# A chunked delta rule ahead of a two-layer projection on one core: merge pieces of two blocks joined, masks moved to GpSimd, a 48-row state update

## The chip, the cores and the metric

The kernel runs on one core of a Trainium2 chip. The metric is device microseconds (us) of one execution; the figure to forecast is that of the changed kernel. Engines are named as in the profile: PE (TensorE, with PEld for its weight loads), DVE (VectorE), ACT (ScalarE), POOL (GpSimd) and SP (SyncE, which issues most transfers).

## The reference

4 batches of 8 heads, 768 steps, head size 48. Per head a 48x48 state is read by the query and then corrected by the key (delta rule). The result, 3072 tokens of 384 numbers, goes through two matrix products with a clipped square between them.

```python
k_n = k / (norm(k) + 1e-06)
for t in range(S):
    y[:, :, t] = einsum('bhd,bhde->bhe', q[:, :, t], state)
    v_old = einsum('bhde,bhd->bhe', state, k_n[:, :, t])
    state = state + beta[t] * einsum('bhd,bhe->bhde', k_n[:, :, t], v[:, :, t] - v_old)
x = y.transpose(0, 2, 1, 3).reshape(B * S, H * D)
h = x @ w_in
g = where(h >= 1, h, where(h <= -1, 0, (h + 1) ** 2 / 4))
out = g @ w_out
```

## The kernel before, in words

The 768 steps are cut into 12 blocks of 64, and blocks go in 6 pairs, G = 0 to 5. Within a block all 32 heads are worked at once (16 units side by side on two halves of the 128 partitions). Per block the kernel makes the Gram matrix of the keys (`gram_k`), inverts the triangular 64x64 system that the Gram matrix and beta define, makes the query Gram matrix and masks it (`gram_q`), and then runs the chain through the state: `chain_r` (the old state's part taken off the values), `chain_u` (the inverse applied), `chain_y` (the output y), `chain_d` (the state's update).

The inverse is made in two steps. DVE solves 32x32 systems of both blocks of a pair together (`solve_whole`, 30 steps of two operations, lines 358 and 360), scales and transposes the result into `XT` and `GG` (`unlanes_whole`, lines 366, 368, 371). PE then joins the 32x32 parts into 64x64 with two products per block (`merge32`): y1 = GG·XT, whose negative ACT writes to `GG`, and x2 = GG·GG, which ACT writes to `XT`.

The other work is the projection, in 102 items. Pair 0 has 22 items, every later pair 16. An item is `up` (9 matmuls of 512 columns into a PSUM buffer h, of which there are two), then ACT's Relu (line 826) and Square (838), DVE's min/max that reads h a last time (840), ACT's cast to ghi (805), DVE's rest glo (806), and `down` (12 matmuls of 384 columns), which runs two items later. So `up` of an item may begin only when line 840 of the item two before has read its h. In this document "the min/max" means line 840.

While the items of pair G run, the inverse and the chain of pair G+1 are woven in. The order is written by hand: `plan(G)` puts pieces for PE into the table `pe` and steps for the other engines into the table `fill`, at times counted in items; each item has two half-steps. In this document "half-step n" counts within the 32 half-steps of one pair's 16 items. A PE piece of an even half-step stands between `up` and `down` of its item, one of an odd half-step behind `down`. Every engine works its list in that order. A piece's PSUM comes from a ring of two banks named `ch`; a piece that needs both waits until the pieces before it have been read out.

In pairs worked by `plan(1)` to `plan(4)` (blocks 4 to 11) the pieces are: `chain_r` of the first block at half-step 5, `gram_q` at 9 and 12, three merge pieces at 17, 18 and 22, `gram_k` of the next pair at 19 and 24, and `chain_u`, `chain_y`, `chain_d`, `chain_r`, `chain_u`, `chain_y`, `chain_d` at 20, 21, 23, 25, 27, 28, 30. The solve begins three half-steps before the pair's own first item.

Of the kernel before, what the change touches and what calls it, by code (L numbers as in the profile page):

```python
# [7 lines left out]
F32 = mybir.dt.float32  # L8
# [5 lines left out]
C = 64  # L14
NP = 4
D = 48
# [24 lines left out]
def delta_rule_moe(ctx: ExitStack, tc: tile.TileContext, kqa, kqb, kv, beta, w, out):  # L41
# [202 lines left out]
    def gram_q(g):  # L244

        x, b_ = Q[g], banks(C)
        for j in range(H):
            for e, f in quarters():
                r, o = slice(f * C, f * C + D), other(e, f) * C
                nc.tensor.matmul(b_[e][o:o + C, j], K[g][r, e * H + j, :], x[r, (1 - f, 1)[e], e * H + j, :], start=True, stop=True)  # L250

        def moved():
            for o in range(2):
                yield x[o * C:o * C + C, o, 0:H], b_[0][o * C:o * C + C], slice(o * C, o * C + C)
            yield x[:, 0, H:NU], b_[1], slice(0, P)

        def evict():
            def raw():
                for a, b, r in moved():
                    nc.scalar.copy(out=a, in_=b)  # L260

            def masks(copied=False):
                for a, b, r in moved():
                    nc.vector.tensor_tensor(out=a, in0=a if copied else b, in1=mask[r, None, :].broadcast_to([r.stop - r.start, H, C]), op=ALU.mult)  # L264
                    yield
            return (raw, masks(True)) if g < 2 else lambda: run(masks())
        return evict

    def norms(n, out):
# [93 lines left out]
    def unlanes_whole():  # L363

        A, gm = S["A"], S["gm"]
        nc.vector.tensor_tensor(out=A, in0=A, in1=gm[:, None, :].broadcast_to([P, 32, 32]), op=ALU.mult)
        yield
        nc.vector.transpose(out=XT[:, :, :, 32:64].rearrange("p g u t -> p t (g u)"), in_=A.rearrange("l c t -> l t c"))
        yield
        for g in range(2):  # L370
            nc.vector.transpose(out=GG[:, g, :, 32:64], in_=XT[:, g, :, 32:64])
            yield
# [44 lines left out]
    def merge32(ga, gb, first=False):  # L417
# [10 lines left out]
        def evict():  # L428
# [3 lines left out]
            if ga is not None:  # L432
# [7 lines left out]
                for r in (0, C):  # L440
                    (nc.vector.tensor_copy if first else nc.scalar.copy)(out=XT[r:r + 32, ga, :, 0:32], in_=XT[r:r + 32, ga, :, 32:64])
        return evict

    def chain_r(g):
        b_ = banks(D)
# [111 lines left out]
    def chain_d(g):  # L557
        b_ = banks(D)
        keys = KV[g].rearrange("p h u d -> p (h u d)")
        for j in range(H):  # L560
            for e, x in quarters():
                r, o, k = slice(x * C, x * C + C), other(e, x) * C, e * H + j
                n = C if e else D
                nc.tensor.matmul(b_[e][o:o + n, j], keys[r, k * D:k * D + n], SU[r, (x, 0)[e], k, :], start=True, stop=True)  # L564

        def moved():
            for f in range(2):
                yield SU[f * C:f * C + D, 1 - f, 0:H], b_[0][f * C:f * C + D]
            yield SU[:, 1, H:NU], b_[1]

        def evict():
            if g == 0:
# [22 lines left out]
    def run(gen, n=99):  # L595
        for _ in range(n):
            if next(gen, 0) == 0:
                break
# [130 lines left out]
    def at(where, G, t, *x):  # L729
        where.setdefault(2 * first[G] + int(round(2 * t)), []).extend(x)  # L730
# [10 lines left out]
    def plan(G):  # L741
# [11 lines left out]
        else:  # L753
# [8 lines left out]
            t, n = (MERGE / 2 + 7 - FT - HALF, 31 + 2 * HALF - MERGE) if G == 1 else (-1.5, 17)  # L762
# [12 lines left out]
        chain(G, M + 1.5, a)  # L775
        if G < NS - 2:
            if G:
# [119 lines left out]
```

## Time and profile before

| | before |
|---|---|
| three runs | 593.45, 595.01, 601.75 us |
| median of them | 595.01 us |
| the profiled execution | 594.22 us |
| its span, first to last instruction | 592.5 us |
| mean granted clock of TensorE | 0.991 |
| PE, DVE, ACT, POOL busy | 574.1, 393.6, 327.3, 32.9 us |

The span is what the rows below are measured in, counted from its start; 1.7 us lie around it. A busy PE is not PE at its peak, since matmuls are pipelined: what a stretch of PE costs is read here from one start to the next start. In the timeline neighbouring rows of one line and form are merged, and the mean granted clock close to 1 means that nearly all of the span ran at 2.4 GHz.

### The profile page before, as it was taken

What the parts mean: (1) busy time and instruction counts of PE and PEld (TensorE: products, weight loads), DVE (VectorE), ACT (ScalarE), POOL (GpSimd) and SP (SyncE); (2) the same over time, 40 slices, a digit from 0 to 9 for tenths busy, and PEclk for the clock granted to TensorE, in tenths of its full rate; (3) what the DMA queues carried; (4) which work ended last, traced back from release to release, by engine and by line L of the source; (5) the groups of instructions that cost most, each with busy time, mean ns of one, the idle gap of its engine ahead of it and who ended that gap; (6) DMA issues with size and microseconds to landing.
All of it is one profiled execution on the core that took longest, in us unless ns stands there. A gap on an engine that the chain in (4) does not pass through costs nothing.

```text
span 592.5 us, 21657 instructions
## 1 busy us (share of the span) xinstructions
PE 574.1 (97%) x9585; PEld 498.0 (84%) x9585; DVE 393.6 (66%) x827; ACT 327.3 (55%) x587; POOL 32.9 (6%) x67
## 2 busy tenths in 40 slices
PE   8898899999999999999999999999999999999996
PEld 6677788789978888888888898888888888899986
DVE  5977999854689934699924699924699924323332
ACT  4648876467544385534385544385544374454443
POOL 6200010000020000010000010000010000000000
PEclk9988999999999999999999999999999999999999
DMA  5674766100343011144011144001143000020001
GB/s 146 195 254 147 202 225 198 56 5 15 93 106 97 1 32 47 37 110 116 10 25 45 36 113 114 15 22 44 36 111 90 1 3 16 15 55 1 0 2 53
DMA packets 32302, 42.77 MB, mean 72 GB/s; under 512 B 7056, under 2 KB 26768, under 8 KB 32208
## 3 DMA queue, kind: packets, MB, share of 16 engines
q1 hardware_dynamic: 31216, 40.41, 23.8%
q8 instruction: 75, 1.23, 0.9%
q0 software_dynamic: 576, 0.57, 0.4%
q10 hardware_dynamic: 416, 0.39, 0.2%
q14 instruction: 19, 0.16, 0.1%
HBM read 34.47 MB, written 4.72 MB: 66 GB/s over the span
## 4 chain that ended last, share of the span: by engine, by line
PE 51%; issue 29%; DVE 11%; ACT 4%; SPq 2%; DMA 1%; POOL 1%; ACTq 0%; POOLq 0%; DVEq 0%
PE h L691 18%; PE o L706 17%; PE ch L491 3%; PE ch L237 2%; PE ch L449 1%; PE ch L465 1%; PE o L165 1%; ACT GG L439 1%; PE ch L426 1%; DVE glo L806 1%; PE ch L250 1%; PE ch L564 1%; PE ch L424 1%; DVE wt L208 1%; DVE pr L347 1%
## 5 line engine op out<-in xcount | busy, mean ns | idle before, releaser
L691 PE MATMUL h<-xb,wt 128*128 128x512 f32 (+1 forms) x918 | 223.1, 386 | 3.8 <-DVE s L840 1.9
L706 PE MATMUL o<-wt,ghi 128*128 128x384 f32 x768 | 200.3, 342 | 0.5 <-issue 0.5
L691 PEld LDWEIGHTS h<-xb,wt 128*128 128x128 f32 x918 | 161.5, 188 | 37.0 <-DVE s L840 2.4
L706 PEld LDWEIGHTS o<-wt,ghi 128*128 128x128 f32 x768 | 137.2, 188 | 7.6 <-issue 0.7
L805 ACT CAST ghi<-s 128x512 fp32r<-128x512 f32 (+1 forms) x102 | 60.9, 597 | 131.6 <-DVE s L840 119.0
L840 DVE SCALAR_TENSOR_TENSOR s<-s,h 128x512 f32<-128x512 f32 (+1 forms) x102 | 66.4, 651 | 95.2 <-ACT s L838 95.2
L706 PE MATMUL o<-wt,glo 128*128 128x384 f32 x384 | 129.3, 337 | 0.4 <-DVE glo L806 0.4
L826 ACT ACTIVATE s<-h,half 128x512 f32<-128x512 f32 (+1 forms) x102 | 67.5, 662 | 61.0 <-PE h L691 60.5
L806 DVE TENSOR_TENSOR glo<-s,ghi 128x512 fp32r<-128x512 f32 (+1 forms) x102 | 66.8, 655 | 43.1 <-ACT ghi L805 42.9
L706 PEld LDWEIGHTS o<-wt,glo 128*128 128x128 f32 x384 | 72.1, 188 | 1.0 <-DVE glo L806 1.0
L838 ACT ACTIVATE s<-s 128x512 f32<-128x512 f32 (+1 forms) x102 | 62.2, 610 | 2.4
L358 DVE TENSOR_TENSOR pr<-A 128x30 f32<-128x30 f32 (+14 forms) x120 | 39.5, 329 | 7.0 <-POOL A L323 5.1
L360 DVE TENSOR_TENSOR A<-A,pr 128x30 f32<-128x30 f32 (+14 forms) x120 | 39.8, 332 | 4.4
L165 PE MATMUL o<-wx 128*128 128x512 f32 x87 | 27.8, 464 | 1.5 <-DVE tiny L175 1.5
L491 PEld LDWEIGHTS ch<-Q,SU 64*64 64x64 f32 (+3 forms) x1056 | 22.6, 135 | 3.7 <-ACT ghi L805 1.5
L491 PE MATMUL ch<-Q,SU 64*64 64x64 f32 (+3 forms) x1056 | 24.8, 222 | 0.0
L165 PEld LDWEIGHTS o<-wx 128*128 128x128 f32 x87 | 18.2, 220 | 5.7 <-DVE tiny L175 1.5
L323 POOL TENSOR_SCALAR_AFFINE_SELECT A<-A 128x1024 f32<-128x1024 f32 x4 | 5.1, 1265 | 297.6 <-DMA xb<-X 255.1
L264 DVE TENSOR_TENSOR Q<-ch,mask 64x512 f32<-64x512 f32 (+1 forms) x30 | 20.6, 687 | 0.5
L474 ACT COPY SU<-ch 64x384 f32<-64x384 f32 (+1 forms) x30 | 14.3, 476 | 6.6 <-PE ch L465 6.3
L439 ACT ACTIVATE GG<-ch 32x512 f32<-32x512 f32 x22 | 12.9, 589 | 8.0 <-PE ch L424 7.7
L579 DVE TENSOR_TENSOR SU<-ch,SU 48x384 f32<-48x384 f32 (+1 forms) x27 | 15.0, 555 | 3.4 <-PE ch L564 3.0
(157 smaller groups left out, 553.9 us busy)
## 6 DMA issues: line engine op xcount, KB each, us to landing
wt<-in_w_dram SPq DMA_DIRECT2D x16, 768.0 KB, 5.7
out_dram<-wx SPq DMA_DIRECT2D x44, 96.0 KB, 2.2
KV<-in_kv_dram SPq DMA_DIRECT2D x36, 96.0 KB, 2.6
KV<-in_kv_dram SPq DMA_DIRECT2D x72, 48.0 KB, 2.3
KV<-in_kv_dram SPq DMA_DIRECT2D x12, 192.0 KB, 2.8
xb<-X SPq DMA_DIRECT2D x60, 32.0 KB, 2.0
K<-in_kqb_dram SPq DMA_DIRECT2D x12, 128.0 KB, 2.7
Q<-in_kqb_dram SPq DMA_DIRECT2D x12, 128.0 KB, 2.7
```

The source lines that it names most:

```text
L165: nc.tensor.matmul(warm_ps, warm[:, 0:P], warm, start=True, stop=True)
L264: nc.vector.tensor_tensor(out=a, in0=a if copied else b, in1=mask[r, None, :].broadcast_to([r.stop - r.start, H, C]), op=ALU.mult)
L358: nc.vector.tensor_tensor(out=pr, in0=A[:, 0:n, j:j + 1].broadcast_to([P, n, m]), in1=A[:, j:j + 1, j + 1:32].broadcast_to([P, n, m]), op= ...
L360: nc.vector.tensor_tensor(out=A[:, 0:n, j + 1:32], in0=A[:, 0:n, j + 1:32], in1=pr, op=ALU.add)
L491: nc.tensor.matmul(yy[i][o * C:o * C + C, e, p], SF[rows, u:u + C], w_[rows, x, k, :], **how)
L691: nc.tensor.matmul(h[:, cols(bs)], WT[f][:, 0, x, k * P:(k + 1) * P], XB[G][:, y, k, cols(bs)], start=(n == 0), stop=(n == 8))
L706: nc.tensor.matmul(oacc[G, k], (ghi, glo)[x][:, k * P:(k + 1) * P], WT[f][:, 1, y, :], start=(new and n == 0), stop=(left[G, b] == 0 and n ...
L805: nc.scalar.copy(out=ghi[:, c], in_=s[:, c])
L806: nc.vector.tensor_tensor(out=glo[:, c], in0=s[:, c], in1=ghi[:, c], op=ALU.subtract)
L826: nc.scalar.activation(out=s[:, c], in_=h[:, c], func=AF.Relu, bias=mid, scale=0.5)
L838: nc.scalar.activation(out=s[:, c], in_=s[:, c], func=AF.Square)
L840: nc.vector.scalar_tensor_tensor(out=s[:, c], in0=s[:, c], scalar=1.0, in1=h[:, c], op0=ALU.min, op1=ALU.max)
```

## The change

For pairs 2 to 5 (blocks 4 to 11) the three merge pieces become two, `merge_first` for y1 of both blocks and `merge_second` for x2 of both, at half-steps 16 and 18; each takes one PSUM bank, and the two blocks' results lie in different quarters of its partitions. The read-out of the first block goes to ACT and that of the second to DVE. What `merge32` did to the left part of `XT` (zeros by POOL, a copy by ACT) is now done for both blocks at once in `corners`, behind the big transpose of `unlanes_whole`. The solve is squeezed by one half-step (16 half-steps in place of 17; 14 in place of 15 where G = 1), and the steps of `unlanes_whole` come one half-step earlier. For blocks 4 to 11 the query Gram matrix is copied out by ACT and masked in place by POOL with four selects, in place of three DVE multiplications that did both. For blocks 2 to 10 `chain_d` loads 48 weight columns everywhere in place of 48 for one half of the heads and 64 for the other, and the state is then added in four DVE operations of 48 rows in place of two of 48 and one of 128.

```diff
+            def later():
+                raw()
+                for a, b, r in moved():
+                    for c in range(r.start, r.stop, C):
+                        y = x[c:c + C, ...]
+                        nc.gpsimd.affine_select(out=y, in_=y, pattern=[[0, H], [1, C]], ...)
-            return (raw, masks(True)) if g < 2 else lambda: run(masks())
+            return (raw, masks(True)) if g < 2 else lambda: run(masks()) if g < 4 else later()
...
         nc.vector.transpose(out=XT[:, :, :, 32:64]..., in_=A...)      # unlanes_whole
+        corners()
         yield
...
+    def merge_first():
+        y1 = ps.tile([P, NU, 32], F32, **acc())
+        for u in range(NU):
+            for g in range(2):
+                for r in (0, C):
+                    nc.tensor.matmul(y1[r + 32 * g:r + 32 * g + 32, u], GG[r + 32:r + 64, g, u, 0:32], XT[r + 32:r + 64, g, u, 32:64], start=True, stop=True)
+        def evict():
+            ...  # GG[r:r + 32, g, :, 0:32] = -y1: ACT for g = 0, DVE for g = 1
+    def merge_second():
+        ...  # x2 of both blocks from GG[r:r + 32], read out by ACT (g = 0) and DVE (g = 1)
+    def corners():
+        for r in (0, C):
+            nc.gpsimd.memset(XT[r + 32:r + 64, :, :, 0:32], 0.0)
+            nc.scalar.copy(out=XT[r:r + 32, :, :, 0:32], in_=XT[r:r + 32, :, :, 32:64])
...
-                n = C if e else D                                     # chain_d
+                n = C if e and g < 2 else D
...
-            yield SU[:, 1, H:NU], b_[1]
+            if g < 2:
+                yield SU[:, 1, H:NU], b_[1]
+            else:
+                for f in range(2):
+                    yield SU[f * C:f * C + D, 1, H:NU], b_[1][f * C:f * C + D]
...
-            t, n = (..., 31 + 2 * HALF - MERGE) if G == 1 else (-1.5, 17)   # plan: solve
+            t, n = (..., 30 + 2 * HALF - MERGE) if G == 1 else (-1.5, 16)
-            for j, t in enumerate((7, 7.5, 8, 8)):                    # plan: unlanes_whole
+            for t in (6.5, 7, 7.5, 7.5):
...
-        for j, x in ((0, (0, None)), (0.5, (1, 0)), (2.5, (None, 1))):
-            at(pe, G, M + j, lambda x=x: merge32(*x))
+        if G:
+            at(pe, G, 8, merge_first)
+            at(pe, G, 9, merge_second)
+        else:
+            ...  # as before
```

What this does to the engines' lists is shown at three places of the pair that `plan(3)` works. The first is DVE around the last item of the pair before (half-steps 30 and 31), where `A` and `pr` are the solve, `SU` is the state and `s<-s,h` is the min/max. Before:

```order
L358 TENSOR_TENSOR pr_5727<-A_5534 128x130
L360 TENSOR_TENSOR A_5534<-A_5534,pr_5727 128x5x26
L579 TENSOR_TENSOR SU_171<-ch_5683,SU_171 48x384 x2
L579 TENSOR_TENSOR SU_171<-ch_5684,SU_171 128x384
L840 SCALAR_TENSOR_TENSOR s_5681<-s_5681,h_5671 128x512
L358 TENSOR_TENSOR pr_5747<-A_5534 128x150
L360 TENSOR_TENSOR A_5534<-A_5534,pr_5747 128x6x25
```

And now:

```order
L366 TENSOR_TENSOR pr_5736<-A_5543 128x130
L368 TENSOR_TENSOR A_5543<-A_5543,pr_5736 128x5x26
L366 TENSOR_TENSOR pr_5739<-A_5543 128x150
L368 TENSOR_TENSOR A_5543<-A_5543,pr_5739 128x6x25
L629 TENSOR_TENSOR SU_171<-ch_5692,SU_171 48x384 x2
L629 TENSOR_TENSOR SU_171<-ch_5693,SU_171 48x384 x2
L894 SCALAR_TENSOR_TENSOR s_5690<-s_5690,h_5680 128x512
```

The solve step of 6x25 and one more state addition now stand ahead of the min/max.

The second is DVE in half-steps 13 to 16, from the min/max of the pair's item 6 on; `XT` and `GG` are the transposes of `unlanes_whole`. Before, and then now:

```order
L840 SCALAR_TENSOR_TENSOR s_6119<-s_6119,h_6109 128x512
L358 TENSOR_TENSOR pr_6178<-A_5534 128x58
L360 TENSOR_TENSOR A_5534<-A_5534,pr_6178 128x29x2
L358 TENSOR_TENSOR pr_6181<-A_5534 128x30
L360 TENSOR_TENSOR A_5534<-A_5534,pr_6181 128x30
L806 TENSOR_TENSOR glo_6192<-s_6119,ghi_6191 128x512
L366 TENSOR_TENSOR A_5534<-A_5534,gm_5621 128x1024
L840 SCALAR_TENSOR_TENSOR s_6205<-s_6205,h_6195 128x512
L368 STREAM_TRANSPOSE XT_173<-A_5534 128x32x32
```

```order
L894 SCALAR_TENSOR_TENSOR s_6139<-s_6139,h_6129 128x512
L374 TENSOR_TENSOR A_5543<-A_5543,gm_5630 128x1024
L860 TENSOR_TENSOR glo_6211<-s_6139,ghi_6210 128x512
L376 STREAM_TRANSPOSE XT_173<-A_5543 128x32x32
L894 SCALAR_TENSOR_TENSOR s_6224<-s_6224,h_6214 128x512
L380 STREAM_TRANSPOSE GG_172<-XT_173 128x16x32 x2
L860 TENSOR_TENSOR glo_6248<-s_6224,ghi_6247 128x512
L466 TENSOR_SCALAR GG_172<-ch_6263 32x16x32 x2
```

The big transpose now stands ahead of the min/max of item 7, and DVE has a read-out of `merge_first`.

The third is ACT over the items 6 to 8; `Q` is the query Gram matrix. Before, and then now:

```order
L826 ACTIVATE s_6119<-h_6109,half_165 128x512
L838 ACTIVATE s_6119<-s_6119 128x512
L805 CAST ghi_6191<-s_6119 128x512
L826 ACTIVATE s_6205<-h_6195,half_165 128x512
L838 ACTIVATE s_6205<-s_6205 128x512
L805 CAST ghi_6223<-s_6205 128x512
```

```order
L880 ACTIVATE s_6139<-h_6129,half_165 128x512
L260 COPY Q_5726<-ch_6141 64x512 x2
L260 COPY Q_5726<-ch_6142 128x512
L892 ACTIVATE s_6139<-s_6139 128x512
L859 CAST ghi_6210<-s_6139 128x512
L880 ACTIVATE s_6224<-h_6214,half_165 128x512
L488 COPY XT_173<-XT_173 32x32x32 x2
L892 ACTIVATE s_6224<-s_6224 128x512
L859 CAST ghi_6247<-s_6224 128x512
```

The copies out of PSUM stand ahead of item 6's Square, and those of `corners` ahead of item 7's.

## Rows read from the trace of the kernel before

**Rows 1.** Busy us in two stretches: length, PE, PEld, DVE, ACT, POOL, clock, DMA.
```profile
341.00:383.00 42.00, 42.00 (x386) 37.56 (x386) 40.11 (x94) 17.76 (x31) 2.41 (x6) 1.00 0.30 81
385.00:403.00 18.00, 17.82 (x445) 14.88 (x438) 5.33 (x11) 14.94 (x28) 0.00 (x0) 1.00 0.08 19
```

**Rows 2.** Timeline of PE, an item without pieces: start us, us, instruction.
```profile
347.17 2.25 PE L691 MATMUL h<-xb,wt 128*128 128x512 f32 x9
349.25 0.51 PE L706 MATMUL o<-wt,ghi 128*128 128x384 f32 x2
```

**Rows 3.** Timeline of PE, first two merge pieces of the same pair.
```profile
384.45 1.20 PE L424 MATMUL ch<-XT,GG 32*32 32x32 f32 x64
385.58 2.34 PE L691 MATMUL h<-xb,wt 128*128 128x512 f32 x9
387.85 0.21 PE L424 MATMUL ch<-XT,GG 32*32 32x32 f32 x1
...
389.07 0.62 PE L706 MATMUL o<-wt,ghi 128*128 128x384 f32 x2
```

**Rows 4.** Groups by form, PE in 398.5 to 400.7, a chain_y: count | busy, mean ns.
```profile
L491 PE MATMUL ch<-Q,SU 128*64 128x64 f32 x16 | 1.1, 225 | 0.0
L491 PE MATMUL ch<-Q,SU 112*64 112x64 f32 x16 | 1.1, 225 | 0.0
```

**Rows 5.** Groups by form, PE in 406.4 to 407.6, a chain_d.
```profile
L564 PE MATMUL ch<-SU,KV 64*64 64x48 f32 x32 | 1.1, 220 | 0.0
L564 PE MATMUL ch<-SU,KV 64*48 64x48 f32 x32 | 0.9, 208 | 0.0
```

**Rows 6.** Timeline of PE, merge and gram_k pieces of several pairs.
```profile
206.54 1.20 PE L424 MATMUL ch<-XT,GG 32*32 32x32 f32 x64 [0.67 <-DVE XT L368]
...
213.45 0.33 PE L237 MATMUL ch<-K 48*64 48x64 f32 x2
213.93 1.15 PE L237 MATMUL ch<-K 48*64 48x64 f32 x62 [0.16 <-ACT GG L439]
...
302.65 1.49 PE L237 MATMUL ch<-K 48*64 48x64 f32 x64
...
409.80 1.16 PE L237 MATMUL ch<-A 48*64 48x64 f32 x64
```

**Rows 7.** Timeline of DVE at the pair's boundary.
```profile
344.43 1.71 DVE L579 TENSOR_TENSOR SU<-ch,SU 48x384 f32<-48x384 f32 x3
346.05 0.68 DVE L840 SCALAR_TENSOR_TENSOR s<-s,h 128x512 f32<-128x512 f32 x1
346.64 0.31 DVE L358 TENSOR_TENSOR pr<-A 128x150 f32<-128x150 f32 x1
...
347.34 0.33 DVE L358 TENSOR_TENSOR pr<-A 128x168 f32<-128x168 f32 x1
```

**Rows 8.** The min/max on DVE at the other two boundaries.
```profile
257.37 0.68 DVE L840 SCALAR_TENSOR_TENSOR s<-s,h 128x512 f32<-128x512 f32 x1
...
434.93 0.68 DVE L840 SCALAR_TENSOR_TENSOR s<-s,h 128x512 f32<-128x512 f32 x1
```

**Rows 9.** The up that needs it on PE, at the same two.
```profile
258.12 2.33 PE L691 MATMUL h<-xb,wt 128*128 128x512 f32 x9
...
436.24 2.25 PE L691 MATMUL h<-xb,wt 128*128 128x512 f32 x9
```

**Rows 10.** Timeline of DVE ahead of the merges.
```profile
380.13 0.68 DVE L840 SCALAR_TENSOR_TENSOR s<-s,h 128x512 f32<-128x512 f32 x1
380.73 2.35 DVE L368 STREAM_TRANSPOSE XT<-A 128x1024 f32<-128x1024 f32 x1
```

**Rows 11.** Groups by form over the whole span.
```profile
L264 DVE TENSOR_TENSOR Q<-ch,mask 64x512 f32<-64x512 f32 x20 | 13.7, 685 | 0.2
...
L609 ACT COPY GG<-wt 128x1024 f32<-128x1024 f32 x2 | 2.1, 1052 | 0.0
...
L323 POOL TENSOR_SCALAR_AFFINE_SELECT A<-A 128x1024 f32<-128x1024 f32 x4 | 5.1, 1265 | 297.6 <-DMA xb<-X 255.1 <-PE ch L564 42.5
```

More of the change, by code (lines that the diff above doesn't have):

```diff
@@ L265, in masks @@
                     yield
-            return (raw, masks(True)) if g < 2 else lambda: run(masks())
+            def later():
+                raw()
+                for a, b, r in moved():
+                    for c in range(r.start, r.stop, C):
+                        y = x[c:c + C, 0 if r.stop - r.start > C else c // C, (0, H)[r.stop - r.start > C]:(H, NU)[r.stop - r.start > C]]
+                        nc.gpsimd.affine_select(out=y, in_=y, pattern=[[0, H], [1, C]], base=0, channel_multiplier=-1,
+                                                compare_op=ALU.is_gt, fill=0.0)
+            return (raw, masks(True)) if g < 2 else lambda: run(masks()) if g < 4 else later()
         return evict
@@ L442, in merge32, with evict @@
         return evict
+    def merge_first():
[5 more added lines that the diff above has]
+        def evict():
+            for g in range(2):
+                for r in (0, C):
+                    x, y = GG[r:r + 32, g, :, 0:32], y1[r + 32 * g:r + 32 * g + 32]
+                    if g:
+                        nc.vector.tensor_scalar(out=x, in0=y, scalar1=-1.0, scalar2=None, op0=ALU.mult)
+                    else:
+                        nc.scalar.mul(out=x, in_=y, mul=-1.0)
+        return evict
+    def merge_second():
+        x2 = ps.tile([P, NU, 32], F32, **acc())
+        for u in range(NU):
+            for g in range(2):
+                for r in (0, C):
+                    nc.tensor.matmul(x2[r + 32 * g:r + 32 * g + 32, u], GG[r:r + 32, g, u, 32:64], GG[r:r + 32, g, u, 0:32], start=True, stop=True)
+        def evict():
+            for g in range(2):
+                for r in (0, C):
+                    (nc.vector.tensor_copy if g else nc.scalar.copy)(out=XT[r:r + 32, g, :, 32:64], in_=x2[r + 32 * g:r + 32 * g + 32])
+        return evict
+    def corners():
+        for r in (0, C):
+            nc.gpsimd.memset(XT[r + 32:r + 64, :, :, 0:32], 0.0)
+            nc.scalar.copy(out=XT[r:r + 32, :, :, 0:32], in_=XT[r:r + 32, :, :, 32:64])
     def chain_r(g):
@@ L761, in plan @@
             cost, hs = 0, 0
-            t, n = (MERGE / 2 + 7 - FT - HALF, 31 + 2 * HALF - MERGE) if G == 1 else (-1.5, 17)
+            t, n = (MERGE / 2 + 7 - FT - HALF, 30 + 2 * HALF - MERGE) if G == 1 else (-1.5, 16)
             for j in range(1, 31):
@@ L772, in plan @@
             last = 16
-        for j, x in ((0, (0, None)), (0.5, (1, 0)), (2.5, (None, 1))):
-            at(pe, G, M + j, lambda x=x: merge32(*x))
+        if G:
+            at(pe, G, 8, merge_first)
+            at(pe, G, 9, merge_second)
+        else:
+            for j, x in ((0, (0, None)), (0.5, (1, 0)), (2.5, (None, 1))):
+                at(pe, G, M + j, lambda x=x: merge32(*x))
         chain(G, M + 1.5, a)
```

## The prediction

> **What bounds the kernel now.** I read the windows first. In the solve stretch of one pair PE is busy for all of 42.00 us and DVE for 40.11; in the chain stretch PE has 17.82 of 18.00 and DVE only 5.33, with ACT at 14.94 [rows 1]. So PE sets the time and DVE is close behind it while it solves; the granted clock is 1.00, the 2.4 GHz level, in both. Since busy PE is not PE at its peak, I then went through the timeline of PE from start to start, to see which blocks are longer than they need be. A bare `up` takes 349.25 - 347.17 = 2.08 us [rows 2]. From 176 us on nearly every block is as short as that, or longer only by what its neighbouring pieces cost; PE really waits in few places. They are 0.67 us ahead of one merge piece, for the big transpose, and a stop inside `gram_k` of three pairs [rows 6]. So a piece that gets shorter on PE is worth its full length, and any wait that is put in front of `up` is paid in full. The change must be summed by PE's pieces, less the waits that go, plus the waits that come.
>
> **The merges.** The first piece lasts 385.58 - 384.45 = 1.13 us with 64 records (32 products, two records each), the second 389.07 - 387.85 = 1.22 us with 128 (one row of them is shown) [rows 3]. Twice the products cost 0.09 us: the first has only two of the array's small tiles at work, the second four. The `up` between the two pieces takes 387.85 - 385.58 = 2.27 us instead of 2.08 [rows 2, 3], so a piece also stretches its surroundings by 0.19. The third piece, of 64, is like the first. Three pieces are 3.48 + 3 x 0.19 = 4.05 us. If four tiles again work side by side, the two new ones of 128 are 2 x (1.22 + 0.19) = 2.82. Saved: 1.23 a pair, 4.9 us for four pairs.
>
> Do they work side by side? Before, the four tiles had four row groups and shared column groups; now two column groups each share one row group. The nearest row is `chain_y`: its 128-row and 112-row products, which share the rows and differ in columns, each span 1.1 us within the same stretch [rows 4]. One behind the other they would span about half of it each. I take the 1.22; the other end is two tiles at a time, 2 x 1.13 = 2.26 a piece, and is a rival.
>
> **Waits that go.** The transpose comes one half-step earlier, as the merge does, but DVE no longer has six mask operations, 6 x 0.685 = 4.1 us a pair [rows 11], in front of it; the 0.67 should go. `gram_k` takes 1.16 undisturbed, but 213.93 + 1.15 - 213.45 = 1.63 and 1.49 behind the merges, and a third time as in the first [rows 6]: 0.47 + 0.33 + 0.47 = 1.3. It waits for both `ch` banks while ACT reads out x2, y1 and makes the corner copies. Now two ACT and two DVE operations read one bank out at the same time. Together 1.9 us go. I keep 0.1 us in three pairs as a rest, 0.3.
>
> **The state update.** In `chain_d` the 48-column tiles span 0.9 us and the 64-column ones 1.1 [rows 5]; with 48 everywhere the piece ends with the former, 0.2 us sooner. Nine pieces change (blocks 2 to 10). The three of the second blocks at a pair's boundary run into the wait of the next paragraph and I count them there; two fall before 165 us, where other things hold PE, and count half; four are free: 4 x 0.2 + 0.2 = 1.0 us. The price is one more DVE operation: three take 346.05 - 344.43 = 1.62, so 0.54 each [rows 7]. At half-step 23 this delays the second bank of `gram_k` behind it, at most 0.1 us in each of four pairs: 0.4.
>
> **The boundary of pairs, where I expect the loss.** The min/max of the pair's last item frees the h buffer of the next pair's second `up`. It ends at 346.05 + 0.68 = 346.73, and that `up` starts at 347.17 [rows 2, 7]: 0.44 us of room. At the other two boundaries it ends at 258.05 and 435.61, and `up` starts at 258.12 and 436.24 [rows 8, 9]: 0.07 and 0.63. DVE is full here, and its list gets two things in front of this min/max: the solve step of 6x25, which lasted from 346.64 to 347.34, 0.70, and the fourth state addition, 0.54 [rows 7]. That is 1.24 us. With a handoff of 0.07, as at the first boundary, `up` starts later by 1.24, 0.87 and 0.68: 2.8 us. The bounds: nothing, if DVE were to reach the place earlier, for which I see no reason, since the solve starts when the previous block's y is out; and 3 x 1.24 = 3.7 if no room is left. At the boundary into pair 1 the solve's steps keep their place there and DVE later waits for a transfer anyway: nothing.
>
> **Masks and corners.** The copies by ACT fall into its free half of the solve stretch (17.76 busy of 42.00) [rows 1], but stand ahead of item 6's Square, so item 6's min/max must wait for the second `gram_q`. Two copies of 32x1024, about 1.05 each by the nearest row [rows 11], stand ahead of item 7's Square and must wait for the transpose of 2.35. Before, the min/max of item 7 ended at 380.13 + 0.68 = 380.81 and was needed by `up` at 385.58 [rows 3, 10], a cover of 4.8. What is now put before it is 2.35 + 2 x 1.05 = 4.45, less what DVE gains by the masks. By my reckoning DVE can start the transpose about 1.1 us earlier than before, at 379.6, so that it ends at 381.95, the copies at 384.1, Square and min/max (0.63 and 0.68) at 385.4. Pieces before it take nearly the same PE time, and PE itself comes up to 0.9 later at this boundary: some 1.2 us of cover are left. Should it be gone, each us is paid by PE in each of four pairs. `merge_second` waits for the read-out of `merge_first`, which ACT and DVE begin only after that; there about 0.3 us are left. I charge nothing for these two.
>
> The GpSimd masks are four selects of 64x512, estimated at half of 1.265 us each [rows 11], 2.5 us a `gram_q`, ready long before `chain_y` reads them.
>
> **Sum.** -4.9 - 1.9 + 0.3 - 1.0 + 0.4 + 2.8 = -4.3 us. Against the profiled execution's 594.22 us (span 592.5 and 1.7 around it) that is **589.9 us**. The median of the three runs is 595.01 and the lowest 593.45, so this execution stands between them, and I shift nothing for it. The gain is 0.7%.
>
> **Rivals.**
> - The boundary costs nothing: 589.9 - 2.8 = 587.1. For it, DVE's list may be shorter than I count; against it, the room of 0.07 that the trace shows at one boundary.
> - Slower than before: the corners hold up ACT. If DVE gains no lead by the masks, because it stands waiting behind item 6's Square, the transpose begins at 380.2, right behind the scaling, and ends at 382.5; the copies end at 384.6 and the min/max at 385.9. `up` then waits 0.3, and `merge_second` another 1.0, since both read-outs queue behind that min/max. 1.3 us in four pairs is 5.2: 595.1, slower than the 594.2 by 0.9. It decides in this way if the transpose ends over 0.5 us later than the 381.95 above. For it: three engines in a ring, each in order. Against it: the 4.1 us that DVE loses.
> - GpSimd and DVE get in each other's way, so that DVE's lead shrinks by half: 4 x 0.65 more, 592.5. The selects run beside solve steps; the profile has no select beside DVE work, since DVE waits for the only one. The Trainium skill, in "SBUF — State Buffer", section "Who interferes with whom", states that a VectorE instruction with two SBUF inputs contends with a GpSimd instruction that reads SBUF; the solve steps are of that kind, and no run here shows it yet.
> - Column tiles that share rows go one after the other: 2 x (2.26 - 1.22) x 4 = 8.3 more, 598.2. Against it stands [rows 4].
>
> **How the numbers follow.** Forecast (588 to 592) 0.5; no boundary wait (585.5 to 588) 0.17; corners (594 to 597) 0.18; GpSimd (592 to 594) 0.1; tiles in turn (597 to 600) 0.05. The range 586.0 to 595.5 leaves out the lowest part of the second case and the upper part of the last two slow ones, together 0.2. Two per cent, about what a measurement of this kernel can tell from no change, is 11.9 us: 583.1 and 606.9 lie outside all cases, so "same" gets 0.93, faster 0.04, slower 0.03 for what I have not seen.
>
> **What would show it.** In the profile of the changed kernel two merge pieces of 128 records should last 1.2 us each, with `gram_k` behind them at 1.2 rather than 1.6, and `chain_d` 0.9 from start to start rather than 1.1. At each of three boundaries `up` of the next pair's second item should start 0.05 to 0.1 us after the min/max, with a visible stop of about 1 us in PE. If `up` of item 9 or `merge_second` waits for DVE or ACT by over 0.5 us, the corners are the cause. A solve step or glo longer than before beside a select would speak for the GpSimd rival. I am wrong altogether if PE stops at places that I have not named.

## The result, and the profile after

The change made the kernel slower by 0.7%: 600.38 us median of 20 runs (598.43 to 603.56) against 596.49 (593.45 to 601.75) of the kernel before on the same chip, a ratio of 1.0073 with a 95% interval of 1.0053 to 1.0092. I had forecast 589.9, a gain of 0.7%, with a range up to 595.5. The profiled execution of the changed kernel lasted 599.76 us, its span 598.0.

PE's timeline shows where. I measure a pair from the start of its second `chain_r` (half-step 25) to that of the next pair; each of these four stretches holds one set of merges. In before they last 85.03, 89.05, 88.87 and 86.02 us, together 348.97; now 85.71, 90.45, 90.43 and 86.26, together 352.85. The 3.9 us between the sums match the 3.9 us between the medians. (Of the 5.5 us between the two spans, 1.7 stand ahead of the first of these pairs; I leave them out.)

The windows that answer to [rows 1], 5 us later as the pair starts 5 us later, columns as there:

```profile
346.00:388.00 42.00, 40.97 (x452) 35.91 (x454) 37.43 (x83) 20.59 (x35) 7.16 (x10) 1.00 0.31 80
390.00:408.00 18.00, 16.47 (x402) 14.07 (x401) 8.81 (x14) 11.60 (x23) 0.00 (x0) 1.00 0.02 6
```

DVE has 37.43 in place of 40.11 in the solve stretch, as meant, yet PE, which was busy throughout, now stands idle for 1.03 us there and 1.53 in the chain stretch. The clock is at its upper level in both, so these are waits. The first is at the pair's boundary. PE's timeline there, which answers to [rows 2]:

```profile
348.69 0.51 PE L756 MATMUL o<-wt,ghi 128*128 128x384 f32 x2
...
351.98 2.37 PE L741 MATMUL h<-xb,wt 128*128 128x512 f32 x9 [1.03 <-DVE s L894]
```

Before, the same `down` began at 345.07 and the `up` behind it at 347.17 [rows 2], 2.10 us:

```profile
345.07 0.51 PE L706 MATMUL o<-wt,ghi 128*128 128x384 f32 x2
```

Now it takes 351.98 - 348.69 = 3.29 us from start to start, since `up` waits for the min/max. DVE's timeline at the same place (against [rows 7]):

```profile
348.72 0.32 DVE L368 TENSOR_TENSOR A<-A,pr 128x150 f32<-128x150 f32 x1
348.95 2.26 DVE L629 TENSOR_TENSOR SU<-ch,SU 48x384 f32<-48x384 f32 x4
351.24 0.69 DVE L894 SCALAR_TENSOR_TENSOR s<-s,h 128x512 f32<-128x512 f32 x1
```

The solve step of 6x25 and the fourth addition (2.26 for four, 1.62 for three before) stand ahead of the min/max; it ends at 351.93, and PE starts 0.05 later. The other two boundaries have a `down` of 3.29 and 3.23, where it took 2.09 each. This is the loss that I had forecast.

The second idle stretch was not forecast. PE's timeline over the two merge pieces and the `gram_k` behind them (against [rows 3] and [rows 6]):

```profile
387.32 1.29 PE L459 MATMUL ch<-XT,GG 32*32 32x32 f32 x128
388.54 0.62 PE L756 MATMUL o<-wt,ghi 128*128 128x384 f32 x2
...
392.91 0.38 PE L476 MATMUL ch<-GG 32*32 32x32 f32 x6
393.77 1.24 PE L476 MATMUL ch<-GG 32*32 32x32 f32 x122 [0.48 <-DVE GG L466]
394.94 0.62 PE L756 MATMUL o<-wt,ghi 128*128 128x384 f32 x2
...
397.22 0.33 PE L237 MATMUL ch<-K 48*64 48x64 f32 x2
398.59 1.15 PE L237 MATMUL ch<-K 48*64 48x64 f32 x62 [1.04 <-DVE XT L481]
```

`merge_first` takes 388.54 - 387.32 = 1.22 us. `merge_second` starts with 6 of its 128 records, stops, and takes 394.94 - 392.91 = 2.03. `gram_k` begins at 397.22 and the `up` behind it at 399.67: 2.45 us, where the kernel before took 1.59 here (391.35 to 392.94) and an undisturbed `gram_k` takes 1.09 from start to start. Both wait for a read-out by DVE. So it is in the last three pairs, but the last has no `gram_k`. The first of the four differs: `merge_first` still waits for the big transpose, and `merge_second` stops twice and takes 2.71 us in all.

```profile
205.44 1.41 PE L459 MATMUL ch<-XT,GG 32*32 32x32 f32 x128 [0.37 <-DVE XT L376]
```

Then the granted clock falls there, to 0.66 on the mean of 213 to 218 us, and the `down` behind takes 3.85 us in place of 2.3. DVE from the big transpose on, in the third pair again:

```profile
384.04 2.33 DVE L376 STREAM_TRANSPOSE XT<-A 128x1024 f32<-128x1024 f32 x1
389.20 0.69 DVE L894 SCALAR_TENSOR_TENSOR s<-s,h 128x512 f32<-128x512 f32 x1 [2.82 <-ACT s L892]
389.81 1.30 DVE L380 STREAM_TRANSPOSE GG<-XT 128x512 f32<-128x512 f32 x2
391.03 0.65 DVE L860 TENSOR_TENSOR glo<-s,ghi 128x512 fp32r<-128x512 f32 x1
392.30 1.41 DVE L466 TENSOR_SCALAR GG<-ch 32x512 f32<-32x512 f32 x2 [0.63 <-ACT GG L468]
...
396.94 1.39 DVE L481 COPY XT<-ch 32x512 f32<-32x512 f32 x2 [0.60 <-ACT XT L481]
```

And ACT in the same time:

```profile
386.41 2.10 ACT L488 COPY XT<-XT 32x1024 f32<-32x1024 f32 x2 [2.45 <-DVE XT L376]
388.54 0.63 ACT L892 ACTIVATE s<-s 128x512 f32<-128x512 f32 x1
389.98 0.62 ACT L859 CAST ghi<-s 128x512 fp32r<-128x512 f32 x1 [0.81 <-DVE s L894]
390.50 0.68 ACT L880 ACTIVATE s<-h,half 128x512 f32<-128x512 f32 x1
391.09 1.18 ACT L468 ACTIVATE GG<-ch 32x512 f32<-32x512 f32 x2
...
395.75 1.15 ACT L481 COPY XT<-ch 32x512 f32<-32x512 f32 x2
```

Read the two together as one chain: transpose on DVE, corner copies on ACT (2.10 us), Square on ACT, min/max back on DVE, ghi and Relu on ACT, ACT's read-out, and only then DVE's. DVE is free at 391.68 and its data have lain in PSUM since 388.6, yet it starts at 392.30, when ACT's two read-outs of the same bank are over. The wait stands in the view of waits four times for each of the two pieces (sum in us, count, mean):

```profile
DVE GG L466 <- ACT GG L468: 2.5, 4, 0.6
...
DVE XT L481 <- ACT XT L481: 2.4, 4, 0.6
```

The third thing to see is DVE beside GpSimd's selects. Groups over the span (count, busy us, mean ns of one):

```profile
L368 DVE TENSOR_TENSOR A<-A,pr 128x30 f32<-128x30 f32 (+14 forms) x120 | 43.4, 362 | 4.4
L366 DVE TENSOR_TENSOR pr<-A 128x30 f32<-128x30 f32 (+14 forms) x120 | 41.4, 345 | 6.8 <-POOL A L331 4.8
...
L374 DVE TENSOR_TENSOR A<-A,gm 128x1024 f32<-128x1024 f32 x4 | 6.3, 1574 | 0.0
```

### The profile page after: what moved, and what is told of

The parts are those of the page before. It is cut to its first block, busy times and chain, and to the rows that moved or that the text cites. A ratio compares the mean times of both kernels' runs of the same rounds, so it can differ in the third digit from the quotient of the medians.

```text
span 598.0 us, 21704 instructions
## 1 busy us (share of the span) xinstructions
PE 572.6 (96%) x9585; PEld 495.6 (83%) x9585; DVE 403.0 (67%) x828; ACT 328.5 (55%) x587; POOL 53.8 (9%) x91
## 4 chain that ended last, share of the span: by engine, by line
PE 44%; issue 22%; DVE 16%; DMA 6%; ACT 4%; SPq 4%; POOL 2%; POOLq 0%; DVEq 0%; ACTq 0%
PE h L741 17%; PE o L756 15%; DMA wt<-in_w_dram 4%; PE ch L537 3%; DVE s L894 2%; DVE pr L366 2%; DVE A L368 2%; DVE glo L860 2%; PE ch L237 2%; PE ch L511 1%; DVE SU L629 1%; PE ch L250 1%; PE ch L495 1%; DVE wt L208 1%; DMA xb<-X 1%
## 5 line engine op out<-in xcount | busy, mean ns | idle before, releaser
L368 DVE TENSOR_TENSOR A<-A,pr 128x30 f32<-128x30 f32 (+14 forms) x120 | 43.4, 362 | 4.4
L366 DVE TENSOR_TENSOR pr<-A 128x30 f32<-128x30 f32 (+14 forms) x120 | 41.4, 345 | 6.8 <-POOL A L331 4.8
L272 POOL TENSOR_SCALAR_AFFINE_SELECT Q<-Q 64x512 f32<-64x512 f32 x32 | 21.4, 669 | 125.9 <-ACT Q L260 124.6
L165 PE MATMUL o<-wx 128*128 128x512 f32 x87 | 29.0, 479 | 1.5 <-DVE tiny L175 1.5
L629 DVE TENSOR_TENSOR SU<-ch,SU 48x384 f32<-48x384 f32 x36 | 20.0, 554 | 3.9 <-PE ch L610 3.5
L260 ACT COPY Q<-ch 64x512 f32<-64x512 f32 (+1 forms) x27 | 15.7, 583 | 3.6 <-PE ch L250 3.1
```

The costliest lines, as they stand in the source:

```text
L165: nc.tensor.matmul(warm_ps, warm[:, 0:P], warm, start=True, stop=True)
L366: nc.vector.tensor_tensor(out=pr, in0=A[:, 0:n, j:j + 1].broadcast_to([P, n, m]), in1=A[:, j:j + 1, j + 1:32].broadcast_to([P, n, m]), op= ...
L368: nc.vector.tensor_tensor(out=A[:, 0:n, j + 1:32], in0=A[:, 0:n, j + 1:32], in1=pr, op=ALU.add)
L629: nc.vector.tensor_tensor(out=x, in0=y, in1=x, op=ALU.add)
```

## The experiments

**Theory A**: merges and `gram_k` stop because of the chain just read, in which the corner copies stand ahead of the read-outs and DVE's read-out waits for ACT's; the boundary costs 1.1 us three times besides. **Theory B**: GpSimd's selects slow DVE down, and the stops follow from that. **Theory C** (from the second set on): boundary and merges are two places that add up and do not act on each other. All runs follow, with the sum of the four pairs from their profiled execution; 348.97 is before, 352.85 the change. The ratio is to the kernel before on the same chip; its median there lay between 595.55 and 596.63 us, so medians of different sets compare to about 1 us.

| run (edit to the changed kernel) | median us | ratio to before | 95% | pairs us |
|---|---|---|---|---|
| masks on DVE | 605.45 | 1.0175 | 1.0147-1.0203 | 358.78 |
| solve not squeezed | 601.23 | 1.0097 | 1.0068-1.0127 | 353.46 |
| corners later | 595.45 | 0.9994 | 0.9967-1.0022 | 347.64 |
| two PSUM tiles | 600.51 | 1.0082 | 1.0052-1.0113 | 350.50 |
| later, not squeezed | 594.27 | 0.9977 | 0.9954-1.0001 | 347.65 |
| later, two tiles | 593.19 | 0.9957 | 0.9932-0.9982 | 347.96 |
| chain_d of 64 columns | 597.46 | 1.0027 | 0.9995-1.0059 | 351.21 |
| corners split | 593.64 | 0.9959 | 0.9937-0.9981 | 347.39 |
| later, two tiles, 64 columns | 591.27 | 0.9932 | 0.9907-0.9957 | 344.42 |
| split, two tiles, 64 columns | 590.78 | 0.9923 | 0.9896-0.9950 | 344.13 |
| merge alone on before | 600.23 | 1.0080 | 1.0053-1.0107 | 355.68 |
| no selects | 597.90 | 1.0042 | 1.0014-1.0073 | 350.41 |
| two tiles, stream shifted | 596.51 | 1.0004 | 0.9974-1.0034 | 349.41 |
| split, two, 64, shifted | 592.27 | 0.9923 | 0.9892-0.9954 | 344.00 |

### Masks on DVE again

```diff
-            return (raw, masks(True)) if g < 2 else lambda: run(masks()) if g < 4 else later()
+            return (raw, masks(True)) if g < 2 else lambda: run(masks())
```

> Query Grams evicted with their mask by VectorE again, as before the change; nothing else undone. Theory A (the two read-outs of each merge step stand one after the other, and the corner copies stand before them on ScalarE, so that merge_second stops 0.8 us and gram_k behind it 1.3 us in each of the last four pairs; besides, the boundary wait of 1.1 us in three of them): the masks are a small part, VectorE loses about 0.9 us of stretch per pair (A*gm 1.56 back to 1.22, the solve operations of 0.67 back to 0.33) but gets the masks back, some 2.35 us per pair, so the two stops in PE stay above 1.5 us together and the time is 599 to 602 us. Theory B (GpSimd's selects beside VectorE's solve cost the time): the stretch goes, the two stops fall under 1 us together and the time is 595 to 597 us.

Slower still, by more than A had foreseen (599 to 602). With no select on `Q` in the program `merge_second` takes 2.69 to 2.73 us in each pair and `gram_k` 2.4 to 2.6. So the selects do not make the stops. That the masks left DVE is worth 5 us to the changed kernel.

### The solve not squeezed

```diff
-            t, n = (..., 30 + 2 * HALF - MERGE) if G == 1 else (-1.5, 16)
+            t, n = (..., 31 + 2 * HALF - MERGE) if G == 1 else (-1.5, 17)
```

> Only the solve's last half-step is given back (it ends at half-step 17 of the pair again, not 16), so one step fewer of the solve, 0.70 us, stands in front of the min/max at each boundary of pairs. Theory A: the down at the three boundaries falls from 3.25 us to 2.6 to 2.8 (0.7 less, as the room of 0.07 to 0.6 us is used up by the fourth state add alone); 0.5 us x 3 = 1.5 us, time 598.5 to 599.5 us, unless the step now at half-step 17 delays A*gm and with it the two read-outs, which would take it back (600.5). Theory B: no change, 600 to 601 us.

The `down` at the boundary falls to 2.59, by just the 0.70 of one step (2.38 at the last boundary), but `merge_second` grows from 2.03 to 2.70 and the `up` and `merge_first` ahead of it by 0.34. DVE's timeline of this run shows why:

```profile
382.46 0.69 DVE L894 SCALAR_TENSOR_TENSOR s<-s,h 128x512 f32<-128x512 f32 x1 [0.93 <-ACT s L892]
383.07 0.60 DVE L366 TENSOR_TENSOR pr<-A 128x58 f32<-128x58 f32 x1
...
384.45 1.22 DVE L374 TENSOR_TENSOR A<-A,gm 128x1024 f32<-128x1024 f32 x1
```

Item 6's min/max waits for Square, and Square stands behind ACT's copies of the second query Gram, which PE has just made. So the chain starts anew here, tied to PE's `gram_q`. In the changed kernel only the scaling follows; here the last two solve steps as well, 1.4 us (383.07 to 384.45). The squeeze costs 0.7 at the boundary and earns 1.0 (0.67 + 0.34) at the merges; the medians, 0.85 us apart, do not tell the two kernels apart.

### The corner copies later, and apart

Later: `corners()` moves from the second to the third step of `unlanes_whole`, behind item 7's Square. Split: one copy there, the other two half-steps on, behind `merge_first`'s read-out.

```diff
         nc.vector.transpose(out=XT[:, :, :, 32:64]..., in_=A...)
-        corners()
         yield
         for g in range(2):
+            if g == 0:
+                corners()          # split: corners(0) here, corners(C) in one more step at 8.5
             nc.vector.transpose(out=GG[:, g, :, 32:64], in_=XT[:, g, :, 32:64])
             yield
```

> The corner copies on ScalarE are issued one half-step later, behind the Square of item 7 instead of in front of it. Theory A: Square, min/max, ghi and Relu of item 7 go up to 2 us earlier, the first read-outs of merge_first (ScalarE 391.1 in the profile of the changed kernel) about 1 us or more earlier, merge_second no longer stops (2.03 to 1.22 us) or gram_k behind it stops less than 0.7 us (now 1.3); gain 1 to 1.5 us in each of four pairs, time 595 to 597 us. Theory B: nothing moves that PE waits for, 600 to 601 us. If the copies now hold the Relu or the merge read-outs instead, by their full 2.1 us, the time is 601 to 603 us.

> The two corner copies on ScalarE (1.05 us each) apart: the first with the third step of the unpacking (half-step 15), the second two half-steps later, behind merge_first's read-out. Theory A (the 2.1 us of copies in one piece delay the ghi and Relu that PE and the read-out wait for): each single copy fits into ScalarE's room per item, so that merge_second does not stop in any pair (the later corners still had 2.10 us in one of four) and gram_k behind it stops less than 0.7 us; 594 to 595.5 us. If the second copy now delays merge_second's own read-outs: gram_k stops 1 us in each pair, 596 to 598 us.

The first is in A's range, the second a little under it: 4.9 and 6.7 us off, from the lists' order alone. ACT of the run with later copies, in the third pair:

```profile
379.67 0.64 ACT L893 ACTIVATE s<-s 128x512 f32<-128x512 f32 x1
382.11 2.10 ACT L489 COPY XT<-XT 32x1024 f32<-32x1024 f32 x2 [1.81 <-DVE XT L376]
...
385.34 1.19 ACT L469 ACTIVATE GG<-ch 32x512 f32<-32x512 f32 x2
```

Square now runs in ACT's idle time ahead of the copies. From the transpose's end to the first read-out it takes 385.34 - 382.07 = 3.27 us in place of 391.09 - 386.38 = 4.71. `merge_second` takes 1.22 to 1.27 in three pairs and 2.10 in the third (below); `gram_k` still takes 2.43 and 1.96 in two. DVE's read-out waits for ACT's here too, and longer, 0.98 us in each pair:

```profile
386.56 1.41 DVE L467 TENSOR_SCALAR GG<-ch 32x512 f32<-32x512 f32 x2 [0.98 <-ACT GG L469]
```

PE at the second pair's `merge_second`, which stops no more:

```profile
299.51 1.29 PE L477 MATMUL ch<-GG 32*32 32x32 f32 x128
300.73 0.62 PE L757 MATMUL o<-wt,ghi 128*128 128x384 f32 x2
```

So the shared read-out alone does not stop `merge_second`; it does when the corner copies have made the chain late.

### Two PSUM tiles per merge step

```diff
-        y1 = ps.tile([P, NU, 32], F32, **acc())
+        y1 = [ps.tile([P, NU, 32], F32, **acc()) for _ in range(2)]
...
-                    nc.tensor.matmul(y1[r + 32 * g:r + 32 * g + 32, u], ...)
+                    nc.tensor.matmul(y1[g][r + 32 * g:r + 32 * g + 32, u], ...)
```

The read-out and `merge_second` likewise.

> Each merge step's results go to two PSUM tiles, one per block, so that ScalarE's and VectorE's read-outs are of different banks. Theory A with the wait set by the shared bank: VectorE's read-outs no longer wait for ScalarE's (0.60 and 0.63 us in each of four pairs), merge_second's stop goes from 0.8 to about 0.2 us and gram_k's from 1.3 to about 0.1 to 0.7; gain 1.2 us per pair, time 595.5 to 597 us. If the wait comes from the destination (one tile in SBUF written by both engines), the 0.6 us stay and the time is 600 to 601 us. Theory B: no change either, 600 to 601 us.

> Both: two PSUM tiles per merge step, so that the two engines' read-outs lie side by side, and the corner copies one half-step later. Theory A: no stop is left at merge_second (1.22 us in all four pairs) nor at the gram_k behind it (1.09), pairs of 88.4 us where the change alone has 90.4 and the later corners 89.0; time 593 to 594.5 us. If both edits remove the same stop: as the later corners alone, 595 to 596 us.

Alone, the wait is gone from the view of waits, so it came from the shared bank and not from the destination. The time does not follow: 600.51, where A had 595.5 to 597. DVE's read-out in that run, in the third pair, starts in the middle of ACT's two (387.30 to 388.49):

```profile
387.90 1.39 DVE L466 TENSOR_SCALAR GG<-ch 32x512 f32<-32x512 f32 x2
```

`merge_second` takes 1.49 and 1.50 in two pairs, 2.09 in the first, and `gram_k` 1.09 to 1.77, and yet the median did not move; the section on a stop in PE's own stream bears on that. With the corner copies later as well, `merge_second` has 1.22 in three pairs and `gram_k` 1.09 to 1.37, and the kernel is faster than before.

The Trainium skill, in "PSUM — Partial Sum Buffer", section "PSUM bank collisions raise a hardware error", says that two engines may access one bank at the same time if they are in different quadrants of it, 32 partitions each. The two blocks' results here do lie in different quadrants. So by the Trainium skill the wait would be the program's own caution, by bank; no run here shows it, since in none do the two engines read a bank of these pieces at once.

### Parts undone and parts alone

```diff
-                n = C if e and g < 2 else D        # chain_d of 64 columns, one add of 128 rows
+                n = C if e else D
```

> chain_d with 64 columns and one add of 128 rows again, all else as in the change: the fourth state add (0.67 us of VectorE) goes at every piece, PE gets 0.2 us more at each of seven chain_d. Theory A: the down at the boundary falls from 3.29 to about 2.6 us (the other 0.4 is the solve's step), but what PE gains there it loses at merge_second, as with the solve's squeeze undone (2.0 to 2.7 us); net 0 to +1, time 600 to 601.5 us. Theory C (separate waits): 3 x 0.6 us off, 7 x 0.2 on, 600 us, merge_second still 2.0.

> Corner copies one half-step later, and the solve again with its last half-step. Alone, the first gave 595.45 us and the second 601.23 (its down at the boundary fell from 3.29 to 2.59 us, but merge_second stopped 0.7 us longer). Theory A (the stretch from the boundary to merge_second is one chain on VectorE and ScalarE; PE that gets there earlier only stops longer at merge_second as long as that chain is last): with the corner copies out of the chain's way there is some room again, so part of the 0.7 us per boundary stays: merge_second 1.2 to 1.9 us, 593.5 to 595.5 us. Theory C (two separate waits that add up): 3 x 0.7 us come off, merge_second unchanged, 593.0 to 593.5 us.

> The kernel before with the two merge pieces and the corner copies alone: masks on VectorE, the solve's last step and chain_d as before. The prediction's terms for it are -4.9 us for the pieces and -1.9 for waits that go, 589.5 us against 596.4. Theory A: the stops at merge_second (0.8 to 1.5 us) and at the gram_k behind it (1.3 us) stand here too, as they come from the corner copies and the read-outs one after the other, and VectorE has the masks as well; they take back 2.1 to 2.8 us in each of four pairs: 597 to 601 us, no boundary wait (down 2.2 us). Theory B (the stops come from GpSimd's selects): none here, 589 to 591 us.

Undoing `chain_d` alone gives 2.9 us back by the medians (the two intervals just overlap) and 1.6 by the pairs, where the theories expected nothing or 0.4. The boundary's `down` is 2.40, and `merge_second` 2.02 to 2.73, as in the changed kernel: what the boundary gains is not lost at the merges. So my A was too strong, and for this edit C holds. My reading is that the chain to the merges is tied to `gram_q`, so that PE that comes earlier takes the whole chain with it, and that the squeeze undone had lost its gain because it put work behind that tie.

The second run agrees with that and not with C's time: 594.27 lies in A's range, not in C's 593.0 to 593.5. With the corners later the two solve steps behind the tie cost as much again: `merge_second` is 1.25 to 1.40, but `gram_k` 2.44 to 2.46 in all three, and the pairs sum to 347.65, no less than with the later corners alone (the medians differ by 1.2 us with overlapping intervals).

The merge change alone on the kernel before (with the steps of `unlanes_whole` one half-step earlier, as the merges need them) costs 4.0 us, 600.23 against 596.27 on that chip, where the prediction's terms say 6.8 gained. PE of that run:

```profile
394.92 0.33 PE L476 MATMUL ch<-GG 32*32 32x32 f32 x4
395.73 0.24 PE L476 MATMUL ch<-GG 32*32 32x32 f32 x2 [0.47 <-DVE GG L466]
396.45 1.24 PE L476 MATMUL ch<-GG 32*32 32x32 f32 x122 [0.48 <-DVE GG L466]
...
401.27 0.94 PE L237 MATMUL ch<-K 48*64 48x64 f32 x49 [1.04 <-DVE XT L481]
```

`merge_second` stops for each of DVE's two read-outs. No select on `Q`, no squeeze, no smaller `chain_d` is in this kernel: the stops belong to the merge change. The rest of the change is worth nothing on balance, to about 1 us (600.23 and 600.38).

### GpSimd's selects left out

```diff
-            return ... else lambda: run(masks()) if g < 4 else later()
+            return ... else lambda: run(masks()) if g < 4 else raw()
```

> The changed kernel without GpSimd's selects: query Grams from the fifth on stay unmasked, so that part of the computation is left out; ScalarE's raw copies stay. Theory A: VectorE's solve operations beside the selects go back from 0.43 to 0.68 us to 0.33 to 0.35 and A*gm from 1.56 to 1.22, some 1 to 1.5 us of VectorE per pair ahead of the two merges; up to half of that reaches PE: 597 to 600 us, merge_second still stops in most pairs or gram_k behind it by over 0.7 us. Theory B: both stops go, 593 to 595 us.

2.5 us faster by the medians, with intervals that overlap, and 2.4 by the pairs, in A's range. DVE of this run:

```profile
L368 DVE TENSOR_TENSOR A<-A,pr 128x30 f32<-128x30 f32 (+14 forms) x120 | 39.9, 332 | 4.4
L366 DVE TENSOR_TENSOR pr<-A 128x30 f32<-128x30 f32 (+14 forms) x120 | 39.4, 329 | 6.8 <-POOL A L331 4.8
...
L374 DVE TENSOR_TENSOR A<-A,gm 128x1024 f32<-128x1024 f32 x4 | 4.9, 1220 | 0.0
```

The selects cost DVE 3.5 + 2.0 + 1.4 = 6.9 us of work, and PE some 2.4. `merge_second` still stops in all pairs (1.62 to 2.10), `gram_k` too (2.1 to 2.6). B is a real cost beside A's, not in its place.

The Trainium skill's rule that the prediction weighed ("SBUF — State Buffer", "Who interferes with whom") agrees with these rows. The Trainium skill adds there that a GpSimd instruction that only writes does not contend; in the third pair of the changed kernel the memsets of `corners` run from 382.51 to 384.47, and the glo beside them, of two inputs, takes 0.68 us, as glo does elsewhere.

### The cures together

> Two PSUM tiles per merge step and corner copies one half-step later (593.19 us together), and chain_d with 64 columns and one 128-row add again (alone 597.46 against 600.38, its down at the boundary 2.40 us instead of 3.29). Theory A (boundary and merges are two places that each cost; with room made in the second, what the first gives back stays): pairs of 87.8 to 88.0 us, time 590.3 to 591.5 us, under both kernels. If VectorE's chain to merge_second takes the boundary's gain back, as it did with the solve's squeeze undone: merge_second stops again, 593 us.

> As the run before it, but the two corner copies apart (half-steps 15 and 17) instead of both one half-step later. Theory A: 590.3 to 591.5 us too; if the second copy gets in the way of merge_second's read-outs, up to 1 us per pair more, 592 to 595 us.

Both beat both kernels, as A with C expected: 591.27 and 590.78. `merge_second` is 1.22 in three pairs and `gram_k` behind it 1.09 to 1.25 in all three; the `down` at the boundaries takes 2.32 to 2.41, still 0.2 to 0.3 more than in the kernel before. What the split adds over the later copies is not told apart here.

### A stop in PE's own stream

In six kernels, with later or split corners or two tiles, PE stops behind `merge_second` of the third of the four pairs for 0.58 to 2.47 us, and nothing in the trace releases it ("issue"). In a seventh, without the selects, it stops there for 0.40. The changed kernel does not show it, nor the run with later corners and no squeeze. With later corners and two tiles:

```profile
387.04 1.29 PE L477 MATMUL ch<-GG 32*32 32x32 f32 x128
389.55 0.71 PE L757 MATMUL o<-wt,ghi 128*128 128x384 f32 x2 [1.23 <-issue]
```

The windows of that run show the granted clock falling right after:

```profile
387.00:389.50 2.50, 1.32 (x129) 1.00 0.02 7
389.50:393.30 3.80, 3.75 (x12) 0.56 0.02 4
```

The `down` behind it runs close to the 1.2 GHz level (granted clock 0.56) and takes 3.84 us, 1.6 more than usual. The stop does not always bring this: with two tiles alone, behind the longest one (2.47), the clock stays at 1.00 and the `down` takes 2.28. Two kernels issue one query Gram twice, to move what follows in PE's stream:

```diff
-        for j in range(H):                                   # gram_q
+        for j in list(range(H)) * (2 if g == 8 else 1):
```

> Two PSUM tiles per merge step alone, and the matmuls of the query Gram of block 8 issued twice (64 more, the same values again, 1.1 us of PE). If the unexplained stop of 2.47 us behind the third merge_second belongs to the place in PE's stream, it goes from there or moves to another instruction; if it belongs to the work there, it stays at the down behind merge_second. Time: if two tiles alone are worth what the trace showed (1.3 us in each of three pairs, 600.4 - 3.5 + 1.1), 597 to 599 us; if they are worth nothing, 600.5 to 602.5 us.

> The fastest kernel so far (two tiles, split corner copies, chain_d with 64 columns: 590.78 us) with the same 64 further matmuls. If the stop of 0.58 us behind the third merge_second belongs to the place in PE's stream, it goes from there (or shows at another instruction), and the time is 590.8 + 1.1 - 0.6, 591 to 592 us; if it belongs to the work there, it stays and the time is 591.5 to 592.5 us.

In both the stop is gone from that place, and none over 0.3 us appears behind 180 us: it belongs to the place in the stream, not to the work. (The added matmuls also make all that follows 1.1 us later, but in the seven kernels the stop ended at times from 386.6 to 397.7 us, so the time is unlikely to decide.)

Two tiles with the shift are at 596.51, 4.0 us under the same kernel without, though PE has 1.1 us more to do. By the pairs of the profiled executions, which lasted 596.46 and 596.13 us at a granted clock of 0.988 and 0.990, the shift gains 1.1. The rest goes with the clock: on the mean of all runs it is 0.990 against 0.982. Why it was lower without the shift is not shown.

So the tiles alone are worth more than their median says: 3.4 us by the pairs (349.41 against 352.85), and 4.5 if the 1.1 us of added matmuls are taken off. That the shift by itself does nothing for the changed kernel is assumed in this; no run has it. In the fastest kernel, whose stop was 0.58 us, the shift gains nothing (592.27, a little over the 591 to 592 expected).

## Why the prediction was wrong

The step that failed is in "Waits that go": "two ACT and two DVE operations read one bank out at the same time". They do so one after the other, with 0.63 us of wait at `merge_second` and 0.60 at `gram_k` in each of four pairs. The reckoning up to there was close: I had the min/max of item 7 at 385.4 on the clock of before, and it ended at 389.89, which is 384.94 when the 4.95 us by which the pair starts later are taken off; `up` of item 9 did not wait, as forecast. DVE was free at 391.68; with 1.41 for its read-outs it would have been done at 393.1, a stop of 0.2 in place of 0.8 at `merge_second`. With two tiles the stop was 0.27.

A second step failed beside it, in "Masks and corners": "about 0.3 us are left" at `merge_second`, and nothing charged for the corner copies. Without the wait there would still have been a stop of 0.27, so there was no room. The copies stand in the chain with 2.1 us, and behind item 7's Square they cost nothing at `merge_second`, though DVE's read-out then waits 0.98 us for ACT's. Either cure alone takes most of that stop away. At `gram_k` two tiles leave 0.5 to 0.7 us of 1.4, the later copies up to 1.3, and both together at most 0.3.

Over the four pairs, from start to start, the merge pieces went from 14.15 to 13.79 us, the `gram_k` pieces from 7.85 to 9.88, `chain_d` from 9.02 to 7.32, and `up` and `down` from 274.62 to 278.57. Term by term:

- **Merges, -4.9**: a piece without a stop takes 1.22 us, as taken from the row of 128, so the tiles that share rows work side by side and that rival is out. But `merge_second`'s stop took 0.8 back in each of three pairs and 1.5 in the first, which lost 1.6 more by the clock: 5.5 in all.
- **Waits that go, -1.9**: of the 0.67 ahead of the first merge, 0.37 stayed. `gram_k`'s stop went in the first of three pairs; in the other two it grew from 0.33 and 0.5 to 1.4, where I kept 0.1. With the line above this is nearly the whole miss of 8.2 (-4.3 forecast, +3.9 measured).
- **`chain_d`, -1.0 + 0.4**: the pieces take 0.86 in place of 1.08, and `gram_k` behind it 1.27 in place of 1.09, so that 0.18 of each 0.22 is lost where the two meet. PE's timeline in the changed kernel (against [rows 5]):

```profile
411.86 0.94 PE L610 MATMUL ch<-SU,KV 64*48 64x48 f32 x64
412.72 2.37 PE L741 MATMUL h<-xb,wt 128*128 128x512 f32 x9
415.02 1.34 PE L237 MATMUL ch<-A 48*64 48x64 f32 x64
416.30 0.61 PE L756 MATMUL o<-wt,ghi 128*128 128x384 f32 x2
```

  With the boundary's fourth addition the edit costs 1.6 us by the pairs and 2.9 by the medians, where I had it near nothing.
- **Boundary, +2.8**: right in place and mechanism; 3.5 measured (`down` of 3.29, 3.29 and 3.23 in place of 2.09, 2.10 and 2.09).
- **Masks and corners, 0**: right for `up`, wrong for `merge_second`. The rival "the corners hold up ACT" had the place, with 1.3 us per pair at 0.18; it was 2.1. Its condition was not met: the transpose ended at 386.38, 381.43 on the clock of before and so earlier than the 381.95 that I had taken, and `up` did not wait. My own sign for the corners, `merge_second` waiting by over 0.5 us, did come true. The rival nearest in time, tiles in turn at 598.2, was so by luck alone, since a piece takes 1.22. That the copies' place in the ring of three engines matters was shown by moving them: 4.9 us.
- **GpSimd**: I made it a rival at 0.1, worth 2.6 us. It was 2.4 to 2.5, and it came on top of the others: a cost that adds belongs into the sum with its own bounds, not among the cases that exclude each other.

## What to carry to other kernels

When two engines share the read-out of one PSUM bank, give each its own bank, or count the two read-outs one behind the other: here the second waited 0.6 to 1.0 us. A copy that is "free" on a half-idle engine is paid by whatever stands behind it in that engine's list, so place it behind the work that another engine waits for: the same instructions in another place were worth 4.9 us. And ask of each step whether it stands ahead of or behind the point where the chain starts anew from the engine that sets the time (here `gram_q` on PE): two solve steps put behind it cost their time at the merges, while an addition taken away ahead of it was a gain that stayed.

## What the runs showed that I had not expected

- PE can stop for 0.40 to 2.47 us at one place of its stream with nothing to wait for, behind a piece of 128 short matmuls, and in one of the kernels the granted clock then fell to 0.56 for the next 3.8 us. 64 more matmuls ahead made it vanish in two kernels. What it is stays open.
- A solve operation of 128x168 beside a select took 0.66 us in place of 0.33, one of 128x30 0.53 in place of 0.21, and the scaling 1.56 in place of 1.22.
- The runs of one kernel spread with the mean granted clock: the kernel before had 593.6 us at 0.997 and 600.1 at 0.978. In the profiled executions the clock falls mostly in 20 to 60 us (0.87 on the mean there in the kernel before, 1.00 behind it), ahead of everything that was changed.
